# A new hand-listed order of all steps, and a branch hint ahead of the closing branch

## The chip, the cores and the metric

The kernel runs on one core of a Trainium2 chip. The metric is the device time of one execution in microseconds (us); the median of three runs of the kernel before is 583.75 us. Engines are called by the profile's short names: PE is TensorE (its matmuls), PEld its weight loads, DVE VectorE, ACT ScalarE, POOL GpSimd, SP SyncE, which here issues all DMAs.

## What is computed

The reference has two stages. The first is a linear attention with a complex decay, over 4 batches, 8 heads, 768 steps of time and 48 channels:

```python
mag = np.sqrt(a_re * a_re + a_im * a_im)
scale = np.minimum(mag, 0.999) / (mag + 1e-06)
for t in range(S):
    S_re, S_im = ar * S_re - ai * S_im + kv, ar * S_im + ai * S_re
    y[:, :, t] = np.einsum('bhd,bhde->bhe', q[:, :, t], S_re)
```

The second takes y as 3072 tokens of 384 channels through h = x @ w_in (384 to 2048), g = h * sigmoid(1.702 h), and g @ w_out (2048 to 384). All data are float32.

## The kernel before, in words

Time is cut into 12 units of 256 steps (three for each batch), each of two chunks of 128. For a unit, `prepare_part` (from L275 on) turns a into decays and rotations, by scans on DVE and tables on ACT, and multiplies them into q and k (the rotations at L207); DMAs of SP that `remap` issues (L409 to L418) then lay q and k out by heads. `attend` (from L422) is the attention of one unit. Its PE steps are, for each chunk: two **score** steps (L484), whose product DVE masks (L490); two **keys** steps, which transpose k (L499) for a copy on ACT (L502); three **mix** steps (L469), which give the attention's output; and one **z** step (L521), which gives the new state. `moe` (from L586) is the second stage for one group of one or two units: **H** steps (L615) into h_ps, a gate on ACT (L628, L630) and DVE (L632), and **O** steps (L645) into o_ps, whose sum DVE copies out (L661) for a DMA (L664). From the second group on each product of H and O is taken three times, with high and low parts of both sides, and a group has 256 columns (one unit) or 512 (two units). The weights are converted from 64-bit words on the way, at first (`convert`, `split`). Small checks of the inputs (`inspect`, `sign`, from L668) fill free time of DVE. At the end `decide` counts on PE whether all checks held; if one did not, `general()`, a slow general version, runs.

The order of the work is written out by hand. `Plan.add` numbers every step as it is described (1864 steps, with an engine, a planned duration, what it reads and writes). `Plan.order` does not plan: it returns the numbers of the string ORDER, and makes sure that no step stands ahead of one that it depends on. The planned durations therefore change nothing in the program. The loop from L838 issues the steps in that order, so that each engine, and SP's queue, has its own part of the list in the list's sequence, and each waits in it for what its steps read. An ACT table load (L841) is put in wherever the list changes tables.

The count of `decide` is loaded by all engines at L844, and L845 branches:

```python
    fits = nc.values_load(count[0:1, 0:1], ...)
    with tc.If(fits < P):
        general()
```

In the runs here all checks hold, so every engine jumps over `general()`.

Of the kernel before, what the change touches and what calls it, by code (L numbers as in the profile page):

```python
# [15 lines left out]
ENG = mybir.EngineType  # L16
# [4 lines left out]
P = 128  # L21
L = 128
QL = 32
T = 256
# [66 lines left out]
def attention_moe(ctx: ExitStack, tc: tile.TileContext, qk_in, v, a_in, w_in, w_out, qn, kn, vn, an, bn, out):  # L91
# [68 lines left out]
    def d_t(n, fast=1.0):  # L160
        return 0.07 + n * 0.00104 / fast
# [113 lines left out]
    def prepare_part(u, i, a, b, np_, mag, den, rec, sp, th, *keys):  # L275
# [34 lines left out]
        add("DVE", d_t(C) + 0.18 * C / (NR * T), rk("den"), lambda: dve.scalar_tensor_tensor(  # L310
# [111 lines left out]
    def attend(u):  # L422
# [20 lines left out]
        for c in range(2):  # L443
# [50 lines left out]
            def keys(hh, c=c, bank=bank):  # L494
                k_ps, key = bank("K", hh)

                def turn():
                    for j in range(4):
                        nc.tensor.transpose(k_ps[:, j, 0:KD], at(4 * hh + j, 1, c), ident[0:KD, 0:KD])  # L499

                add("PE", 0.27, rk(4 * c + hh), turn, r=hk[c], w=[key], work=0.85)
                add("ACT", a_t(4 * KD) - 0.12, rk(4 * c + hh), lambda: act(  # L502
                    out=kt[hh], in_=k_ps[:, :, 0:KD], func=AF.Copy
                ), r=[key], w=[f"kt{hh}"])
# [11 lines left out]
            def state(grp=None, c=c, vt=vt, reads=reads):  # L516
# [7 lines left out]
                add("PE", 0.56, rk(4 * c + 2.5), zed, r=reads["z"], w=["Z"], work=0.49, cols=E0)  # L524
# [312 lines left out]
    with tc.manual_schedule(engines={ENG.PE, ENG.Activation, ENG.DVE, ENG.Pool, ENG.SP}):  # L837
        for n in order:  # L838
            o = plan.ops[n]
            if o[5] not in (None, cur):  # L840
                nc.scalar.preload_act_table_set(o[5])  # L841
                cur = o[5]
            o[3]()
    fits = nc.values_load(count[0:1, 0:1], skip_runtime_bounds_check_because="it is only compared, never an address")  # L844
    with tc.If(fits < P):  # L845
        general()
# [256 lines left out]
```

## Time and profile before

| what | us |
|---|---|
| median of three runs (581.92, 583.75, 584.99) | 583.75 |
| the profiled execution, its own time | 580.61 |
| its span, first to last instruction | 578.9 |
| what lies around the span | 1.7 |
| first matmul to the last, in the span | 23.8 to 571.8 |
| PE busy, DVE busy, ACT busy | 531.9, 435.6, 337.6 |

A busy PE is not a PE at its peak: matmuls are pipelined, and a step that waits little still shows as busy. How long a step takes is read from the chain of waits, where a row is one piece of the chain with its start, its length and how many matmuls it has.

### The profile page before, as it was taken

How to read it: one execution, taken by the hardware profiler on the slowest of the kernel's cores; microseconds unless marked ns; L12 is line 12 of the kernel's file. 1: busy time of each engine (PE TensorE's matmuls, PEld its weight loads, DVE VectorE, ACT ScalarE, POOL GpSimd, SP SyncE). 2: the span in 40 equal slices, each digit the busy share in tenths (PEclk: the TensorE clock that was granted, in tenths of full speed). 3: DMA queues.
4: the chain of work that ended last, by engine and by line, in shares of the span. 5: the costliest groups of instructions: out<-in, count | busy, mean ns of one | idle time of the engine just before them, and what ended most of it. 6: DMA issues, size and time to landing. Idle time of an engine off the chain costs nothing.

```text
span 578.9 us, 14799 instructions
## 1 busy us (share of the span) xinstructions
PE 531.9 (92%) x6300; PEld 461.0 (80%) x6300; DVE 435.6 (75%) x739; ACT 337.6 (58%) x483; POOL 23.9 (4%) x83
## 2 busy tenths in 40 slices
PE   0369999999999998999999999999999999999995
PEld 0257877999999998988878888888888888888883
DVE  6998998999999998789889786978476734352232
ACT  7856686796978484386947836546854422233230
POOL 3001000001000000000000100000001000000000
PEclk9997999999999999899999999999999999999999
DMA  8556992163465648264372654754523372131011
GB/s 326 167 190 249 287 295 81 32 168 123 89 214 112 215 80 245 57 173 156 85 205 76 159 165 141 165 172 118 131 56 122 103 163 74 51 110 45 29 45 61
DMA packets 31530, 80.12 MB, mean 138 GB/s; under 512 B 4448, under 2 KB 8032, under 8 KB 31456
## 3 DMA queue, kind: packets, MB, share of 16 engines
q1 hardware_dynamic: 31456, 79.09, 46.5%
q8 instruction: 51, 0.84, 0.6%
q14 instruction: 23, 0.19, 0.1%
HBM read 55.44 MB, written 4.72 MB: 104 GB/s over the span
## 4 chain that ended last, share of the span: by engine, by line
PE 63%; DVE 3%; issue 1%; DMA 1%; ACT 1%; SPq 0%; DVEq 0%
PE o_ps L645 26%; PE h_ps L615 25%; PE x_ps L469 5%; PE p_ps L484 4%; PE p_ps L499 1%; PE z_ps L521 1%; DMA out_dram<-osb 1%; DVE qk L207 1%; DVE osb L661 0%; DVE qr L207 0%; DVE s L207 0%; DVE s L333 0%; DVE pm L490 0%; DVE gl L632 0%; ACT s L319 0%
## 5 line engine op out<-in xcount | busy, mean ns | idle before, releaser
L628 ACT ACTIVATE gh<-h_ps 128x512 fp32r<-128x512 f32 x88 | 52.4, 597 | 136.0 <-PE h_ps L615 96.5
L615 PE MATMUL h_ps<-xhi,hiA 128*128 128x512 f32 (+1 forms) x336 | 117.8, 351 | 0.3 <-DVE gl L632 0.3
L615 PE MATMUL h_ps<-xlo,hiA 128*128 128x512 f32 (+1 forms) x336 | 116.1, 345 | 0.0
L615 PE MATMUL h_ps<-xhi,loA 128*128 128x512 f32 (+1 forms) x336 | 116.0, 345 | 0.0
L632 DVE TENSOR_TENSOR gl<-h_ps,gh 128x512 fp32r<-128x512 f32 x88 | 60.0, 685 | 55.5 <-ACT h_ps L630 50.0
L645 PE MATMUL o_ps<-gl,hiU 128*128 128x512 f32 (+1 forms) x336 | 85.5, 353 | 1.3 <-issue 1.3
L645 PE MATMUL o_ps<-gh,hiU 128*128 128x512 f32 (+1 forms) x336 | 84.6, 351 | 0.0
L645 PE MATMUL o_ps<-gh,loU 128*128 128x512 f32 (+1 forms) x336 | 82.4, 344 | 0.0
L841 ACT ACT_TABLE_LOAD x58 | 74.4, 1283 | 1.8 <-PEq L1091 0.8
L615 PEld LDWEIGHTS h_ps<-xhi,hiA 128*128 128x128 f32 x336 | 64.2, 191 | 8.1 <-DVE gl L632 0.5
L615 PEld LDWEIGHTS h_ps<-xhi,loA 128*128 128x128 f32 x336 | 64.1, 191 | 7.7
L615 PEld LDWEIGHTS h_ps<-xlo,hiA 128*128 128x128 f32 x336 | 64.2, 191 | 7.2
L645 PEld LDWEIGHTS o_ps<-gl,hiU 128*128 128x128 f32 x336 | 56.6, 191 | 9.4 <-issue 2.1
L645 PEld LDWEIGHTS o_ps<-gh,loU 128*128 128x128 f32 x336 | 57.6, 189 | 7.8
L645 PEld LDWEIGHTS o_ps<-gh,hiU 128*128 128x128 f32 x336 | 56.6, 189 | 7.5 <-issue 0.4
L490 DVE TENSOR_TENSOR pm<-p_ps,mask 128x512 f32<-128x512 f32 x46 | 31.5, 685 | 29.8 <-PE x_ps L469 19.2
L630 ACT ACTIVATE h_ps<-h_ps 128x512 f32<-128x512 f32 x88 | 51.8, 593 | 0.0
L677 DVE TENSOR_REDUCE fit<-raw_w 128x1 f32<-128x256 f32 x96 | 37.3, 409 | 16.0 <-DMA raw_w<-in_w_out_dram 12.4
L207 DVE TENSOR_TENSOR qk<-qk,s 128x768 f32<-128x768 f32 (+1 forms) x52 | 45.7, 889 | 3.0 <-DMA qk<-in_qk_dram 2.5
L484 PEld LDWEIGHTS p_ps<-qkh 96*32 96x32 f32 x1472 | 33.4, 109 | 13.8 <-issue 10.6
L484 PE MATMUL p_ps<-qkh 96*32 96x128 f32 (+3 forms) x1472 | 38.1, 235 | 6.5 <-issue 5.9
L469 PE MATMUL x_ps<-pm,v 128*32 128x128 f32 x768 | 39.7, 281 | 2.9 <-DVE pm L490 1.6
(96 smaller groups left out, 749.3 us busy)
## 6 DMA issues: line engine op xcount, KB each, us to landing
v<-in_v_dram SPq DMA_DIRECT2D x24, 416.0 KB, 4.1
ri<-in_a_dram SPq DMA_DIRECT2D x11, 768.0 KB, 5.5
qk<-in_qk_dram SPq DMA_DIRECT2D x11, 768.0 KB, 6.4
qkh<-qr SPq DMA_DIRECT2D x22, 288.6 KB, 5.9
qkh<-qk SPq DMA_DIRECT2D x22, 288.6 KB, 4.8
raw<-in_w_in_dram SPq DMA_DIRECT2D x8, 768.0 KB, 6.6
raw<-in_w_out_dram SPq DMA_DIRECT2D x8, 768.0 KB, 5.9
raw_w<-in_w_in_dram SPq DMA_DIRECT2D x24, 256.0 KB, 2.8
```

The lines of the kernel that those rows point to most:

```text
L207: add(en, t, rank, lambda: e.tensor_tensor(out=out, in0=a, in1=b, op=alu), **kw)
L469: mm(x_ps[32 * j : 32 * j + 32, r, :], lhsT=lt, rhs=rt, start=n == 0, stop=n == len(steps) - 1)
L484: mm(ps_[to : to + QL, j, lo:L], lhsT=at(h, 1, c)[:, lo : lo + QL], rhs=at(h, 0, c)[:, lo:L], start=True, stop=True)
L490: add("DVE", d_t(CW), rk(4 * c + hh), lambda: dve.tensor_tensor(out=pm[hh], in0=bank("P", hh)[0], in1=mask, op=ALU.mult), r=[bank("P", hh) ...
L499: nc.tensor.transpose(k_ps[:, j, 0:KD], at(4 * hh + j, 1, c), ident[0:KD, 0:KD])
L615: mm(h_ps[hb][:, k * n_t : (k + 1) * n_t], lhsT=ww[:, r * T + f * P : r * T + (f + 1) * P], rhs=x[:, r, 0:n_t], start=n == 0, stop=n == last)
L628: add("ACT", a_t(CW) - 0.13, rk(s), lambda hb=hb, gb=gb: act(out=high.g(gb), in_=h_ps[hb], func=AF.Silu, scale=SLOPE), r=[f"h{hb}"], w=[f" ...
L630: add("ACT", a_t(CW) - 0.13, rk(s), lambda hb=hb: act(out=h_ps[hb], in_=h_ps[hb], func=AF.Silu, scale=SLOPE), w=[f"h{hb}"], tab=SILU, name ...
L632: add("DVE", d_t(CW), rk(s), lambda hb=hb, gb=gb: dve.tensor_tensor(out=glo[gb], in0=h_ps[hb], in1=high.g(gb).bitcast(F32), op=ALU.subtrac ...
L645: mm(o_ps[c][:, 0:n_t], lhsT=y[:, f * DM + c * P : f * DM + (c + 1) * P], rhs=x[:, k * n_t : (k + 1) * n_t], start=i == 0 and f == 0 and n ...
L677: add("DVE", d_t(CK), rk + 2, lambda x=x, op=op: dve.tensor_reduce(out=f_w[:, x, n : n + 1], in_=weights.looked_at()[:, :, 1], op=op, axis ...
L841: nc.scalar.preload_act_table_set(o[5])
```

## The change

Three things are changed. The string ORDER is another permutation of the same 1864 numbers, so every step is still issued once, with the same operands. Planned durations of three kinds of step are changed (they are read by nothing). And a branch hint is put on PE, SP, DVE and ACT between the last listed step and the load of the count, for the branch that now has the label "end"; POOL has none.

```diff
-        add("DVE", d_t(C) + 0.18 * C / (NR * T), rk("den"), lambda: dve.scalar_tensor_tensor(
+        add("DVE", d_t(C), rk("den"), lambda: dve.scalar_tensor_tensor(
...
-                add("PE", 0.27, rk(4 * c + hh), turn, r=hk[c], w=[key], work=0.85)
+                add("PE", 0.277, rk(4 * c + hh), turn, r=hk[c], w=[key], work=0.85)
...
-                add("PE", 0.56, rk(4 * c + 2.5), zed, r=reads["z"], w=["Z"], work=0.49, cols=E0)
+                add("PE", 0.615, rk(4 * c + 2.5), zed, r=reads["z"], w=["Z"], work=0.49, cols=E0)
...
-        for n in order:
+        for k, n in enumerate(order):
...
+    tc.mark_branch_hint_location("end", "LikelyTaken", (ENG.PE, ENG.SP, ENG.DVE, ENG.Activation))
     fits = nc.values_load(count[0:1, 0:1], skip_runtime_bounds_check_because="it is only compared, never an address")
-    with tc.If(fits < P):
+    with tc.If(fits < P, label="end"):
         general()
...
 ORDER = """
-80 130 0 10 185 169 101 151 15 81 82 83 132 131 84 133 85 89 86 134 2 135 93 3
+80 130 0 5 101 151 10 81 82 83 132 131 84 133 85 89 86 134 2 93 135 3 90 94
...
-1684 1681 1685 1686 1682 1687 1689 1690 1688 1694 1691 1692 1695 1862 1863 1693
+1684 1681 1685 1686 1682 1688 1689 1692 1687 1694 1693 1862 1690 1695 1863 1691
 """
```

The two lists, read as PE sees them, around the attention of unit 5 (the number of PE instructions of a step is behind the colon, matmuls and weight loads together):

```
before: mix:32 score:64 mix:64 mix:32 z:96 score:64 O:6 H:18 H:18 O:12 O:6 keys:8 H:18
after:  mix:32 score:64 mix:64 mix:32 H:18 O:6 H:18 H:18 score:64 z:96 O:12 keys:8 O:6
```

Counted over the lists: a change on PE from a score, mix or z step to an H or O step comes 32 times before and 49 times after (19 and 32 times from where the list has passed 155 us of PE work, about 200 us of the profile). Changes from keys to H or O are 36 in both. Table loads of ACT are 58 before and 54 after. The list keeps the last three O steps, the copies out and the count at its end, in another sequence of the three.

## Rows read from the trace of the kernel before

**Rows 1.** The page, part 1: busy time of PE and DVE, share of the span, instructions.

```profile
PE 531.9 (92%) x6300; PEld 461.0 (80%) x6300; DVE 435.6 (75%) x739; ACT 337.6 (58%) x483; POOL 23.9 (4%) x83
```

**Rows 2.** Busy time of each engine by stretch: the stretch, its length, then busy us (and instructions) of PE, PEld, DVE, ACT, POOL, granted clock of PE, DMA share, GB/s.

```profile
150.00:200.00 50.00, 49.22 (x721) 47.86 (x721) 47.77 (x77) 36.93 (x49) 2.53 (x11) 1.00 0.61 167
200.00:250.00 50.00, 45.59 (x824) 44.48 (x826) 42.60 (x68) 27.35 (x40) 1.10 (x5) 0.97 0.50 128
400.00:450.00 50.00, 50.00 (x547) 41.94 (x546) 33.04 (x60) 32.56 (x45) 1.85 (x5) 1.00 0.39 99
```

**Rows 3.** All waits of PE between 200 and 350 us: what waited, for what, us in total, times, longest. "issue" is time in which PE waited for nothing that the profile shows.

```profile
PE p_ps L484 <- issue: 4.8, 4, 2.6
PE o_ps L645 <- issue: 1.3, 2, 0.7
```

**Rows 4.** Of the waits of PE between 60 and 200 us, the one of this kind.

```profile
PE p_ps L484 <- issue: 1.2, 1, 1.2
```

**Rows 5.** As rows 2, of stretches that each begin and end where a wait of this kind ended. The counts behind PE and PEld, added, are the PE instructions between two such ends.

```profile
215.38:231.37 15.99, 13.41 (x253) 13.16 (x254) 14.63 (x26) 8.66 (x12) 1.10 (x5) 1.00 0.83 245
231.37:247.38 16.02, 14.91 (x256) 14.60 (x257) 10.57 (x17) 6.93 (x12) 0.00 (x0) 0.89 0.29 68
...
322.50:339.40 16.90, 16.35 (x254) 13.60 (x254) 14.24 (x26) 10.48 (x15) 0.78 (x4) 1.00 0.70 188
```

**Rows 6.** The page, part 3: the DMA queue that brings PE's instructions (packets, MB, share).

```profile
q8 instruction: 51, 0.84, 0.6%
```

**Rows 7.** As rows 2, of stretches of 256 PE instructions by start (PE's records counted in order of time, from the end of one such wait back by 256, or on by multiples of it). The first three end with a wait for issue, the last two do not.

```profile
225.90:231.37 5.47, 2.88 (x145) 2.77 (x134) 4.47 (x7) 0.00 (x0) 0.00 (x0) 1.00 0.74 272
319.16:322.50 3.34, 3.03 (x146) 2.89 (x134) 2.04 (x4) 3.30 (x6) 0.40 (x1) 1.00 0.44 96
334.31:339.40 5.09, 4.54 (x140) 3.82 (x129) 4.54 (x9) 0.91 (x2) 0.00 (x0) 1.00 0.69 227
363.59:366.15 2.56, 2.56 (x139) 2.56 (x133) 2.52 (x4) 2.54 (x4) 0.00 (x0) 1.00 0.59 155
416.78:419.46 2.68, 2.68 (x138) 2.68 (x131) 0.97 (x3) 2.65 (x4) 0.00 (x0) 1.00 0.24 89
```

**Rows 8.** The chain of waits, pieces in order of time: start, us, what, matmuls. 200 to 260 us.

```profile
228.10 0.68 PE p_ps L484 x27
228.78 2.59 issue
231.37 0.32 PE p_ps L484 x3
...
232.63 3.16 PE h_ps L615 x18
...
239.02 1.08 PE h_ps L615 x9
```

**Rows 9.** As rows 2: the one stretch after 60 us at a lower granted clock.

```profile
231.39:234.80 3.41, 3.41 (x18) 3.35 (x19) 3.07 (x5) 0.94 (x1) 0.00 (x0) 0.50 0.02 5
```

**Rows 10.** The chain of waits, 296 to 345 us. The piece at 319.44 follows a score step, the one at 332.90 an O step; the score at 318.75 follows an O step, the one at 334.36 a mix step.

```profile
318.75 0.69 PE p_ps L484 x32
319.44 1.32 PE x_ps L469 x48
...
332.90 1.46 PE x_ps L469 x48
334.36 0.56 PE p_ps L484 x32
```

**Rows 11.** The chain of waits, 408 to 460 us: H after keys, a z step, H after O, H after a score step.

```profile
409.31 2.12 PE h_ps L615 x9
...
419.05 0.67 PE z_ps L521 x48
...
422.82 2.04 PE h_ps L615 x9
...
447.03 2.26 PE h_ps L615 x9
```

**Rows 12.** The page, part 6: DMA issues, KB of each, median us from issue to landing.

```profile
v<-in_v_dram SPq DMA_DIRECT2D x24, 416.0 KB, 4.1
...
qkh<-qr SPq DMA_DIRECT2D x22, 288.6 KB, 5.9
```

**Rows 13.** The page, part 5: the table loads of ACT.

```profile
L841 ACT ACT_TABLE_LOAD x58 | 74.4, 1283 | 1.8 <-PEq L1091 0.8
```

**Rows 14.** The branch at L845 and what follows on each engine: duration in ns (least, median, most), first and last start in us.

```profile
L845 SPq EVENT_SEMAPHORE  x8: 17/17/17, 577.0 to 577.5; - x8
...
L845 POOLq COMPARE_BRANCH  x1: 45/45/45, 573.4 to 573.4; - x1
L845 PEldq COMPARE_BRANCH  x1: 4222/4222/4222, 573.4 to 573.4; - x1
...
L845 SPq COMPARE_BRANCH  x1: 45/45/45, 573.5 to 573.5; - x1
...
L845 DVEq EVENT_SEMAPHORE  x1: 21/21/21, 577.1 to 577.1; - x1
```

**Rows 15.** The end in order of time: start, us, engine, line, what.

```profile
571.10 1.69 SPq L664 DMA_DIRECT2D out_dram<-osb  x3
...
572.35 0.13 DVE L714 CAST count<-p_ps 1x1 int32<-1x1 f32 x1
```

152 rows, old and new, of the table ORDER are left out of this document.

## The prediction, on record before the change was run

> **What bounds the kernel now.** I read the page first: PE is busy for 92% of the span and DVE for 75% [rows 1]. A share over the whole span hides stages, so I cut it into stretches. Until about 200 us both are full: DVE works 47.8 of 50 us there; later it works 42.6 and then 33.0 of 50 [rows 2]. So up to 200 us a stop of PE may cost nothing, as DVE holds the pace as well; from 200 us PE alone sets the end.
>
> Then the waits of PE. Between 200 and 350 us it waits, over 150 ns at a time, for no engine and no DMA: the whole list is "issue", 4.8 + 1.3 = 6.1 us in six stops [rows 3]. There is one more before, of 1.2 us [rows 4]. Such a row names no culprit, so I counted PE's instructions from the end of one stop to the end of the next: 507, 513 and 508 [rows 5], that is twice 256, but for a few that belong to the sequencer and aren't counted. PE stops at every so many instructions, not at a step. And a queue of its own brings PE's code in 51 packets of 0.84 MB, 16 KB each, one for each 256 of the 12600 instructions [rows 1, 6]. I take the stops to be late code: a block is through before the next is there. The block ahead of a stop was short: 5.47 us with its stop of 2.59 us, or 3.34 and 5.09 us [rows 7].
>
> **What the list does to the blocks.** I give each PE step the length that its pieces have in the chain (a score step 0.69 us for 64 instructions, 48 matmuls of mix 1.32 for 96, z 0.67 for 96, H 2.04 or 1.08 for 18 [rows 8, 10, 11]) and slide a window of 256 instructions over both lists. Before, the least is 2.5 us, and by chance of phase about 9 blocks would lie under 4.2 us. After, nothing past the start-up (the first 16 us of PE work) is under 4.9 us. Attention steps that stood together now have H and O steps between them.
>
> **The sum.** From 200 us on, where PE bounds:
> - The six stops: 4.8 + 1.3 = 6.1 us go [rows 3]. The longest block with its stop took, from 200 us on, 5.47 us [rows 7], so against 4.9 some 0.6 us could stay, at the one densest place. Bounds 5.5 to 6.1; I take **-6.1**, since few blocks are that short.
> - Resuming. The score step that was cut by the stop of 2.59 us took 0.68 + 0.32 us [rows 8], one that wasn't took 0.69 [rows 10]: 0.3 us. Four of the six stops cut a score step [rows 3]: **-1.2**.
> - The clock. Right after the stop of 2.59 us the granted clock is 0.50, the 1.2 GHz level, for 3.41 us [rows 9], and 18 matmuls of H take 3.16 us [rows 8] for twice 1.08. So the dip costs between 1.0 us and half of 3.41, 1.7. PE had stood still before it; without the stop I expect no dip: **-1.4**.
> - The price: more changes between small and large matmuls. A mix step takes 1.46 us behind an O step, 1.32 behind a score step; a score 0.69 behind O, 0.56 behind a mix [rows 10]: 0.14 to enter. H takes 2.26 us behind a score step and 2.04 behind O [rows 11]: 0.22 to leave. Each further excursion costs 0.36 us. From 200 us on the list has 32 in place of 19: 13 x 0.36 = **+4.7**. Keys steps, at 2.12 against 2.04 [rows 11], are as many as before. Bounds: 13 x 0.22 = 2.9, and 17 x 0.36 = 6.1 if the early ones count too.
>
> Up to 200 us: the stop of 1.2 us [rows 4] and four more excursions (1.4 us) lie beside a DVE that is 96% busy [rows 2]. The DVE work listed ahead of each 25 us of PE work is less by 0.1 to 1.3 us than before, summed with DVE's own durations. I take **-0.6**, bounds -2.5 and +2.
>
> The moved queues. SP issues the remaps in sequence with the loads. From the second unit on, the PE work listed between a unit's last remap and the first step that reads it is at least 7.6 us after (6.5 before), and a remap lands 5.9 us after its issue [rows 12]: covered; if the list is early by 2 us more, PE waits for the difference, unit by unit. The first unit's v loads move behind its q and k loads and around its first remap; a load lands in 4.1 us [rows 12], the z step that reads it comes after the remaps, which take as long: 0, at worst +2 at the start, within the bound above. POOL only swaps neighbouring edge fills and copies, which wait for DVE: 0. ACT drops 4 table loads of 1.28 us [rows 13], 5.1 us on an engine busy 58% [rows 1]: 0 on the path. The planned durations are read by nothing: 0. The last three O steps change places among themselves, the copy out of the last still closes: 0.
>
> The end. After the branch at 573.4 us PE's takes 4.22 us, where POOL's, without a long jump, takes 45 ns; SP's next instruction comes at 577.0, 3.5 us after its branch, DVE's at 577.1 [rows 14]. I read this as waiting for the code behind `general()`. A hint can't wait less than its head start. SP's stands behind its last issue (571.10 + 1.69 = 572.8), DVE's behind the cast (572.35 + 0.13 = 572.5) [rows 15]; their branches are at 573.5 or just before. That is 0.7 to 0.9 us. PE and ACT could gain more, but then SP and DVE are late next: SP has eight waits of its own behind the branch [rows 14]. **-0.8**; bounds 0 (the trace has no hint, and its own issue is of the order of 45 ns) and -3.5.
>
> Together -6.1 - 1.2 - 1.4 + 4.7 - 0.6 - 0.8 = **-5.4 us**. The profiled execution took 580.61 us, which would become 575.2. It lies 3.1 us under the median of 583.75, whose runs spread over 3 us. Taken from the median: **578.4 us**.
>
> **A rule against it.** Every stop here is at a multiple of 256 instructions [rows 5]. The Trainium skill, in "Runtime: NRT & Kernel Launch", section "Instruction fetch mechanics", says the contrary: crossing such a block is mostly hidden, as instructions are dispatched slower than they are filled in. By that rule the stops would be something else and stay, and the sum is that of the first rival. The trace disagrees where blocks are short, by 0.3 to 2.6 us at each stop.
>
> **Rivals.**
> 1. *The stops stay* (slower). Closeness doesn't decide; the code's packets come late behind other DMA traffic, wherever the block boundary then lies. For it: two blocks of 2.56 and 2.68 us passed without a stop, and DMAs were busy 0.24 to 0.59 there, against 0.44 to 0.74 at the three stops [rows 7]. Against it: no block with a stop took over 5.47 us there [rows 7], so a later boundary must be later still to show. Then 6.1, 1.2 and 1.4 us aren't won and the excursions are paid: +4.7 - 0.6 - 0.8 = +3.3, 587.1 us. It decides if fetches take over 7 us. Chance 0.11.
> 2. *The excursions eat it.* A lone z step, which now often stands between H and O steps, has no row before that shows its price; if each excursion costs 0.6 us rather than 0.36, early ones included, 17 x 0.6 = 10.2 stands against 6.1 + 1.2 + 1.4 + 0.8 = 9.5: +0.7, 584.4 us. Against it: z is as short as score, and its neighbours are the same. With parts of this, no change that shows: 0.23.
> 3. *The early part gains too.* If DVE's stretch up to 200 us gets shorter by the bound of 2.5, and the hint saves 3.5: -6.1 - 1.2 - 1.4 + 4.7 - 2.5 - 3.5 = -10.0, 573.8 us. Against it: DVE's work is the same. Chance 0.16.
>
> That the hint does nothing would move the sum to -4.6, within the forecast.
>
> **How the numbers follow.** The forecast, -3 to -8 us, has 0.50. About 0.5% (2.9 us) is what a measurement of this kernel can tell from no change. Faster by more: the forecast and rival 3, 0.66; within it: rival 2, 0.23; slower: rival 1, 0.11. The range reaches from beyond rival 3 to rival 2: 573.0 to 584.5 us leaves out rival 1 and a tail of the third, less than 2 in 10.
>
> **What would show it.** In the changed kernel's profile: waits of PE for issue between 200 and 350 us under 1 us in all; no stretch at clock 0.50 behind them; more pieces of H and O at 2.26, and of mix at 1.46 us; SP's first wait behind the branch about 0.8 us nearer to it, PE's branch far under 4.2 us. The prediction is wrong if waits for issue stay at 256 instructions, if new waits of PE for DVE or ACT of over 3 us in all appear after 200 us, or if the first 200 us hold over 2 us more or less PE work.

## The result, and the profile after

The changed kernel takes 568.47 us (median of 4 runs, 567.57 to 570.37), the kernel before 583.23 (4 runs, 581.92 to 584.99): a ratio of 0.975, 95% interval 0.971 to 0.979, 14.8 us less. The forecast was 5.4 us less, with a range down to 573.0 us: the direction was right, but the gain was 2.7 times the forecast and the time lay below the range. The profiled execution took 567.6 us for 580.61, its span 565.8 for 578.9. So 13.1 us can be followed through the two traces; the rest is that the profiled run of before lay further below its median.

Busy time hardly moved against [rows 1, 6], though the span shrank by 13 us. Parts 1 and 3 of the page after:

```profile
PE 532.5 (94%) x6300; PEld 457.1 (81%) x6300; DVE 433.2 (77%) x739; ACT 333.3 (59%) x479; POOL 23.9 (4%) x83
...
q8 instruction: 50, 0.82, 0.6%
```

**The stops** are nearly gone. From 200 to 350 us the list of PE's waits, six stops of 6.1 us before [rows 3], is empty. From 60 to 200 us it has one stop, for the 1.2 us of [rows 4]:

```profile
PE p_ps L484 <- issue: 0.5, 1, 0.5
```

From 60 us to PE's last step no stretch has a granted clock under 1.00, where before had 3.41 us at 0.50 [rows 9].

**The price of excursions** came as worked out. The chain of waits after, 406 to 425 us (start, us, what): z behind H takes 0.81 where it took 0.67 behind a score step [rows 11], mix 1.46, and O behind attention 2.26 or 2.27 (9 matmuls of H behind another large step take 2.04).

```profile
404.78 2.04 PE h_ps L615 x9
406.82 0.81 PE z_ps L521 x48
407.63 0.82 PE p_ps L484 x29
408.45 2.27 PE o_ps L645 x9
...
420.35 1.46 PE x_ps L469 x48
421.81 0.56 PE p_ps L484 x32
422.37 0.44 PE x_ps L469 x16
422.81 2.26 PE o_ps L645 x9
```

**The early part**, which I had at -0.6 us, is where much of the rest is. Busy time by stretch as in [rows 2], first the kernel before, then after:

```profile
30.00:60.00 30.00, 24.71 (x387) 20.27 (x380) 26.44 (x41) 18.35 (x26) 2.40 (x5) 0.89 0.67 241
60.00:110.00 50.00, 46.80 (x546) 39.81 (x545) 46.38 (x68) 36.86 (x50) 1.38 (x5) 1.00 0.57 174
110.00:200.00 90.00, 89.01 (x1293) 86.60 (x1293) 86.75 (x133) 68.48 (x91) 5.37 (x15) 1.00 0.55 149
```

```profile
30.00:60.00 30.00, 26.18 (x401) 20.87 (x399) 28.16 (x44) 21.69 (x30) 3.71 (x7) 0.94 0.74 227
60.00:110.00 50.00, 49.26 (x582) 42.70 (x580) 48.73 (x72) 39.99 (x53) 1.85 (x5) 1.00 0.61 201
110.00:200.00 90.00, 89.50 (x1346) 86.59 (x1348) 88.14 (x138) 67.04 (x91) 3.69 (x15) 1.00 0.53 145
```

The third busy figure is DVE's: 159.57 of 170 us before, 165.03 after. DVE stood 10.4 us in these stretches and now stands 5.0. What stood shows in the waits of PE, ACT and DVE from 24 to 110 us, of the kernel before (kt is the transposed k, pm the masked scores, raw the weights as they are loaded):

```profile
PE z_ps L521 <- ACT kt L502: 2.4, 1, 2.4
PE x_ps L469 <- DVE pm L490: 1.6, 1, 1.6
PE x_ps L469 <- ACT x L527: 1.3, 1, 1.3
PE p_ps L484 <- issue: 1.2, 1, 1.2
PE p_ps L499 <- ACT kt L502: 1.0, 1, 1.0
```

```profile
ACT raw L225 <- DMA raw<-in_w_out_dram: 5.7, 1, 5.7
```

```profile
DVE qk L207 <- DMA qk<-in_qk_dram: 2.5, 1, 2.5
DVE pm L490 <- PE p_ps L484: 1.9, 2, 1.7
```

and after:

```profile
PE x_ps L469 <- DVE pm L490: 1.6, 1, 1.6
PE x_ps L469 <- DVE st L440: 0.9, 1, 0.9
...
PE z_ps L521 <- ACT kt L502: 0.6, 1, 0.6
```

```profile
ACT raw L225 <- DMA raw<-in_w_out_dram: 0.3, 1, 0.3
```

Before, ACT stood 5.7 us in front of a weight load (f4, the fifth of 16; L225), with the copies of kt behind it in its queue; z waited 2.4 us for kt, mix 1.3 us for the copy behind it, and PE ran at half its clock from 43.66 us on, for 6.83 us, 5.53 of them busy. After, the clock was half earlier and for 3.42 us, all busy. Half of the difference in busy time is 1.1 us, my estimate of what the clock has in the early gain. Before, then after:

```profile
43.66:50.49 6.83, 5.53 (x72) 4.49 (x70) 6.73 (x11) 3.07 (x6) 2.14 (x5) 0.50 0.67 255
```

```profile
37.92:41.34 3.42, 3.42 (x69) 2.66 (x69) 2.93 (x5) 0.85 (x1) 1.57 (x3) 0.50 0.67 225
```

**The end.** The rows that answer to [rows 14], and the hint's own:

```profile
L846 SPq EVENT_SEMAPHORE  x8: 17/17/17, 563.8 to 564.4; - x8
...
L846 PEldq COMPARE_BRANCH  x1: 393/393/393, 563.2 to 563.2; - x1
...
L846 SPq COMPARE_BRANCH  x1: 70/70/70, 563.3 to 563.3; - x1
```

```profile
L1100 SPq BRANCH_PREFETCH_HINT  x1: 60/60/60, 0.8 to 0.8; - x1
...
L1100 PEldq BRANCH_PREFETCH_HINT  x1: 50/50/50, 0.9 to 0.9; - x1
```

PE's branch takes 0.39 us for 4.22, SP goes on 0.5 us behind its branch for 3.5, and the span ends 2.6 us behind it for 5.5. The hint is not where the source line stands, between the last step and the load of the count: it is ahead of every listed step, at 0.8 to 0.9 us, 562 us ahead of the branch.

To put the 13.1 us in their places I matched the traces step by step: for each list, when did PE begin the step that has so much listed PE work ahead of it in the list (with the lengths of the prediction)? Below, "a work of 62" means the step that has 62 us of PE work ahead of it. The experiments' traces stand beside them; what was changed in each is told with it.

```
PE work listed ahead, us     0     15     30     62    150    200    300    508  | span
before                    23.8   52.0   67.0  105.0  196.3  254.5  359.9  571.3  | 578.9
after                     23.6   47.9   64.3   98.3  190.7  242.8  347.0  561.1  | 565.8
early part new            23.4   46.1   62.5   96.9  189.9  247.3  353.7  565.1  | 572.6
later part new            23.1   51.4   66.4  104.0  195.2  247.2  351.4  564.5  | 572.2
one conversion moved      23.1   48.5   64.5  104.6  195.5  252.2  359.4  570.8  | 578.3
old list, padded          23.3   50.9   65.9  101.3  193.9  246.0  349.0  560.6  | 568.8
combination               23.5   47.9   63.9   98.3  190.7  242.6  346.3  558.5  | 563.3
```

After is 5.6 us ahead at a work of 150 (196 us in before), 10.2 at PE's end and 13.1 at the span's: early part -5.6, from there on -4.6, end -2.9. The prediction had -0.6, -4.0 and -0.8. The early gain is larger than the spread of runs: PE reaches a work of 150 at 194 to 199 us in the four traces whose early part is the old one, untouched, and at 190 to 193 us in the ten with the new one.

In the experiments' series the runs of before spread by 1.5 to 2.2%, and the ratios leave out runs more than 1.5% above a kernel's fastest, so medians of all runs stand beside them.

### The profile page after: what moved, and what is told of

It is laid out like the page before. It is cut to its first block, busy times and chain, and to the rows that moved or that the text cites. A ratio compares the mean times of both kernels' runs of the same rounds, so it can differ in the third digit from the quotient of the medians.

```text
span 565.8 us, 14819 instructions
## 1 busy us (share of the span) xinstructions
PE 532.5 (94%) x6300; PEld 457.1 (81%) x6300; DVE 433.2 (77%) x739; ACT 333.3 (59%) x479; POOL 23.9 (4%) x83
## 4 chain that ended last, share of the span: by engine, by line
PE 75%; DVE 12%; DMA 5%; ACT 3%; issue 2%; SPq 1%; POOL 0%; DVEq 0%; ACTq 0%; POOLq 0%
PE o_ps L645 31%; PE h_ps L615 30%; PE x_ps L469 6%; PE p_ps L484 4%; PE z_ps L521 2%; PE p_ps L499 2%; DMA qk<-in_qk_dram 1%; DVE qk L207 1%; DMA raw<-in_w_out_dram 1%; DVE s L367 1%; DMA raw_w<-in_w_out_dram 1%; DVE valU L232 1%; DVE valU L229 1%; DVE s L349 1%; DVE valA L229 1%
## 5 line engine op out<-in xcount | busy, mean ns | idle before, releaser
L469 PE MATMUL x_ps<-pm,v 128*32 128x128 f32 x768 | 37.8, 275 | 1.7 <-DVE pm L490 1.6
L484 PE MATMUL p_ps<-qkh 96*32 96x128 f32 (+3 forms) x1472 | 36.3, 236 | 0.7 <-issue 0.5
```

The source lines that it names most:

```text
L469: mm(x_ps[32 * j : 32 * j + 32, r, :], lhsT=lt, rhs=rt, start=n == 0, stop=n == len(steps) - 1)
L484: mm(ps_[to : to + QL, j, lo:L], lhsT=at(h, 1, c)[:, lo : lo + QL], rhs=at(h, 0, c)[:, lo:L], start=True, stop=True)
```

## The experiments

**The hint alone.** The old list, with the hint.

```diff
+    tc.mark_branch_hint_location("end", "LikelyTaken", (ENG.PE, ENG.SP, ENG.DVE, ENG.Activation))
...
+    with tc.If(fits < P, label="end"):
```

> The old list with the hint alone. The two traces put the new kernel's last instruction 2.6 us behind the branch, before it was 5.5 us. If the hint alone does that, this run is 2.9 us under the kernel before (580.3 for 583.2) and PE's closing branch takes about 0.4 us in place of 4.2. If the prediction's reasoning holds, that a hint gives no more than its head start, 0.8 us. If the end is shorter because of the new list's last steps, nothing.

578.28 us for 581.23; ratio 0.996 (0.993 to 1.000). The span ends 2.7 us behind the branch (577.0 to 579.7), PE's branch takes 398 ns. The trace shows 2.8 us at the end, as the first theory says; the times alone barely tell the gain from nothing.

**The new list alone.** The changed kernel without the hint.

```diff
-    tc.mark_branch_hint_location("end", "LikelyTaken", (ENG.PE, ENG.SP, ENG.DVE, ENG.Activation))
...
-    with tc.If(fits < P, label="end"):
+    with tc.If(fits < P):
```

> The new list without the hint. If list and hint add up, 2.9 us above the kernel after, that is 11 to 12 us under the kernel before (571 to 572), with the closing branch at 4.2 us on PE again. The prediction's sum gave the list alone -4.6 us (578.6).

571.15 us for 581.23; ratio 0.983 (0.979 to 0.987), 10.1 us less. PE's branch takes 4478 ns again. Within the spread of the runs, list and hint add up.

**Two halves of the list.** Here and below the new string is written short, as it is made from the two lists.

```diff
-ORDER = old
+ORDER = new[:350] + [n for n in old if n not in new[:350]]   # the early part new
+ORDER = old[:349] + [n for n in new if n not in old[:349]]   # the later part new
```

> The new list's first 350 steps (63 us of PE work, up to about 100 us), then the rest in the old list's sequence; no hint. Theory: the start-up and the early part gain by themselves, and the gain is kept to the end, as it is PE's time and not covered by DVE: -5 to -6 us (577 to 578), and the six stops of 200 to 350 us are all there (about 6 us of waits for issue). Rival, the prediction's: DVE holds the pace up to 200 us, so the early gain is eaten again: -0.6 us, within 0.3% of before. Then the early gain of the full change would come from the later steps' places.

> The old list's first 349 steps, then the rest in the new list's sequence; no hint. Theory: only what the prediction's sum has for the stretch from 200 us on, -4 to -5 us (578.5), and the start-up's 6.8 us at the half clock and its wait of PE for kt of 2.4 us are as before. Rival: the later steps carry the whole gain, -10 us or more. Waits of PE for issue from 200 us on under 1 us under both, if closeness makes the stops.

Early part new: 574.69 us; ratio 0.991 (0.987 to 0.995), medians 6.5 us apart. PE is 8.1 us ahead at a work of 62 and still 6.2 at its end, with all six stops there (200 to 350 us):

```profile
PE p_ps L484 <- issue: 4.7, 4, 2.6
PE o_ps L645 <- issue: 1.9, 2, 1.0
```

Later part new: 576.52 us; ratio 0.993 (0.990 to 0.997), medians 4.7 us apart, no wait for issue from 200 to 350 us. So the early gain exists by itself, is as large as the later one, and DVE does not eat it: the claim that DVE holds the pace falls. The later part is close to what the sum said (-4.0).

**One conversion moved.** Is it the 5.7 us wait of ACT?

```diff
-... 192 191 193 ... 181 187 ... 196 ... 197 24
+... 192 191 193 ... 181 187 ... 196 ... 197 21 24   # 21: ACT's copy of raw f4, 24: DVE's last step of f4
```

> The old list with one conversion moved: ACT's copy of the raw weights f4, which waits 5.7 us for its load ahead of the copies of kt, goes behind the attention's output copies (steps 191, 193, 304, 290, 181, 197), and the DVE step that reads it right behind it. Theory: this is the bigger part of the start-up's gain. PE's wait for kt of 2.4 us goes and much of the 6.8 us at the half clock; the PE work of the first 15 us is done 2.5 to 4 us sooner (at 48 to 49.5 us for 52.0), and what is left at the end is -2 to -4 us (579 to 581 for 583). Rival: the new list's other moves in the start-up make it, DVE's and SP's order above all: under 1 us, as ACT's wait only moves elsewhere.

582.30 us for 583.04; ratio 1.007 (1.003 to 1.010): no gain. The start-up does what the theory said: 3.5 us ahead at a work of 15, kt's wait 0.3 us. But PE then waits elsewhere, and by a work of 62 only 0.4 us is left. PE's waits from 24 to 200 us:

```profile
PE o_ps L645 <- DVE valU L232: 4.7, 1, 4.7
PE x_ps L469 <- DVE pm L490: 4.6, 2, 2.9
```

valU, converted weights of w_out, waits for the load f10. Here it is issued at 62.1 us, 1.0 us sooner than before, but needs 8.4 us to land where before it needed 6.1 (the load's row, before and here):

```profile
raw<-in_w_out_dram SPq DMA_DIRECT2D x1, 768.0 KB, 6.1
```

```profile
raw<-in_w_out_dram SPq DMA_DIRECT2D x1, 768.0 KB, 8.4
```

The load that takes f4's buffer (f8) is not what is late: it lands at 52.6 us for 51.9. And f10 is later still in a trace where no step was moved (the hint alone: 10.0 us to land, PE's wait 4.5 us). So the theory is half right: that wait costs what it seemed to in the start-up, but removing it alone gains nothing, by 12 runs. Where the 3.5 us went is not shown.

**Loads or steps.** Which half of the early part is it?

```diff
-ORDER = old
+ORDER = old, with steps 0 to 79 (weight loads, conversions) at the new list's places   # loads alone
+ORDER = old, with the rest of new[:350] in the new sequence, steps 0 to 79 as in old   # steps alone
```

> The old list, in which the 16 weight loads of the start and their 64 conversion steps stand where the new list has them (by the work listed ahead of them); 7 other steps move with them. Theory: the early gain comes from the lead between a load and its first conversion (f4: 3.4 us of PE work between its issue and ACT's conversion in the old list, 10.3 in the new one), so that neither ACT nor DVE stands for a late load: -4 to -6 us (577 to 579), PE's waits for kt and valU under 1.5 us in all. Rival: the sequence of the attention's and the decay's steps makes it; under 1.5 us here. The six stops of 200 to 350 us are there in both.

> The other half: the first 350 steps in the new list's sequence, but for the weight loads and their conversions, which stand where the old list has them. Theory of the leads: no gain, within 1.5 us of before, with a wait of ACT or DVE for raw of 4 us or more and PE behind it. Rival: -4 to -6 us.

Neither theory holds: both halves lose. Loads alone: 594.35 us for 582.11, ratio 1.020 (1.015 to 1.024). Steps alone: 585.90, ratio 1.007 (1.003 to 1.011). Waits of PE and DVE from 24 to 110 us in the first,

```profile
PE o_ps L645 <- DVE valU L232: 2.7, 1, 2.7
PE h_ps L615 <- DVE valA L232: 2.7, 1, 2.7
PE x_ps L469 <- ACT x L527: 2.5, 1, 2.5
```

```profile
DVE qk L207 <- DMA qk<-in_qk_dram: 4.8, 1, 4.8
```

and of ACT and DVE in the second:

```profile
ACT raw L225 <- DMA raw<-in_w_out_dram: 4.8, 1, 4.8
```

```profile
DVE valA L226 <- DMA raw<-in_w_in_dram: 3.4, 1, 3.4
```

Each half brings waits of 2.5 to 4.8 us that the whole new list doesn't have. My reading is that four raw buffers, one queue of loads and three engines that take their work in sequence have to fit each other. What is shown is that neither half has the early gain alone; which few of the displaced steps would do is open.

**The old list, padded.** Is a stop tied to the steps or to the block's end?

```diff
+        for _ in range(32):
+            mm(h_ps[0][:, 0:1], lhsT=ident, rhs=ident[:, 0:1], start=True, stop=True)
```

> The old list, with 32 one-column matmuls on PE at the start, where PE waits for its first data anyway: 128 instructions more (matmuls and weight loads), so that every block boundary lies 128 instructions earlier in the list. Theory of blocks of 256 that come late: no stop is left at the six old steps; the short blocks are then those that begin at 179, 210, 225, 243 and 333 us in the trace of before (2.50, 2.53, 2.79, 2.56 and 2.69 us long), and stops of 0.5 to 2.8 us stand at the end of three to five of them; about 3 to 8 us in all, the time within 3 us of before. Rival, closeness itself (the steps that follow too closely make PE's queue run dry, wherever a block ends): the stops stay at the same steps with the same lengths.

571.89 us for 583.04; ratio 0.991 (0.987 to 0.995), so 5 us by the ratio and 11 between the medians; the spans of the two traces are 10.1 us apart, 8.3 of it from a work of 150 on (366.7 us to PE's end for 375.0). For that stretch the sum had 6.1 + 1.2 + 1.4 = 8.7 us for the stops and what follows them, and 0.75 us of stops is left. Waits for issue from 60 to 350 us, and PE's counts from the end of the first stop to that of the second (1146 + 1145: nine times 256, but for 13 not counted):

```profile
PE p_ps L484 <- issue: 1.0, 1, 1.0
PE x_ps L469 <- issue: 0.8, 1, 0.8
```

```profile
179.26:242.01 62.75, 62.00 (x1146) 60.83 (x1145) 59.71 (x99) 39.43 (x58) 2.66 (x10) 1.00 0.58 158
```

No stop is left at the six old steps, so the rival falls. Counted through (PE's records in order of time, the sequencer's included), all 52 stops past 60 us in the 18 traces end at a number that leaves 193 when divided by 256, padded or not. How many stops there would be I had wrong: two, not three to five, and a gain of 5 to 11 us was in neither theory. The phase of the old list was an unlucky one.

**Fewer transfers.** The loads of 90 of the 96 weight blocks that are looked at left out (`inspect`, L668 on).

```diff
-        add("SP", 0.8, rk, lambda: dma(
+        add("SP", 0.8, rk, lambda: n % 16 == 0 and dma(
```

> The old list with 90 of the 96 loads of the weights' checks left out (most blocks of the weights are then not checked; the reductions run on what lies there). DVE, ACT and PE do the same work, the DMAs carry less from 200 us on. The prediction's first rival (code comes late behind other transfers): the waits for issue of 200 to 350 us fall from 6.1 us to under 2. Theory that a block needs some 5 us to come, whatever else is moved: at least 4 us of them stay.

584.36 us for 583.04; ratio 1.011 (1.003 to 1.019). The DMA share from 250 to 350 us fell from 0.53 and 0.51 to 0.42 and 0.38, and the stops from 200 to 350 us stay, 6.0 us:

```profile
PE p_ps L484 <- issue: 4.8, 4, 2.1
PE o_ps L645 <- issue: 1.2, 2, 0.8
```

Only three of them lie behind 250 us, though, 2.4 us for 1.6 before; from 200 to 250 us the share is 0.50 in both, so the other three, 3.6 us for 4.4, say nothing. From 250 us on, then, fewer transfers do not bring the code sooner. What makes it late can be narrowed down: the packets of PE's code queue, one for each block in sequence, for some of the shorter blocks of three traces.

```
kernel     block, us   stop, us   next code packet starts: behind block's start / ahead of its end, us
before       2.55        0           -0.93 / 3.49
before       3.05        0            0.34 / 2.70
before       3.75        0.75         1.51 / 2.24
before       4.03        1.10         0.85 / 3.18
before       5.47        2.59         3.01 / 2.46
padded       3.28        0            0.55 / 2.73
padded       4.41        0.98         1.90 / 2.51
padded       5.30        0.75         2.70 / 2.60
after        6.29        0.50         3.89 / 2.40
```

The same holds in all 18 traces, which have 828 block ends past 60 us. At the 52 with a stop, PE goes on 2.2 to 3.2 us behind the packet's start, and without the stop it would have been through the block at most 2.6 us behind it. At the 776 without a stop, the packet started at least 2.2 us ahead of the block's end. That is what shows the stops to be late code. No block of over 5.8 us of its own stopped PE, but 69 blocks under 5 us passed, as their packet came early. What delays a packet's start is open.

**The new list, padded.** Is the new list lucky too? The changed kernel, with the same two lines of padding.

> The kernel after with the 128 instructions of padding. Closeness theory: in the new list no 256 PE instructions past the start-up take under 4.9 us wherever a block begins, so waits of PE for issue past 60 us stay under 1.5 us in all and the time within 1.5 us of the kernel after (567 to 570). Rival: the new list is only lucky in its phase, as the padded old list was; then 3 us or more of such waits, 571 or more.

566.89 us for 582.11; ratio 0.974 (0.970 to 0.978). No wait for issue over 0.15 us past 60 us at all. In the two phases tried the new list has 0.5 and 0 us of stops past 60 us, the old one 7.2 and 1.7.

**The combination**: three of the edits above together.

```diff
-ORDER = old
+ORDER = new[:350] + [n for n in old if n not in new[:350]]   # and the padding, and the hint
```

> The new list's first 350 steps, then the old sequence, with the 128 instructions of padding at the start and with the hint. If the parts add up: early part -5.5 to -6.5, blocks -7 to -9 (what the padded old list gained from 150 us on), hint -2.9, and no further excursions between small and large matmuls to pay for: -15 to -18 us against the kernel before (565 to 568), which is level with the kernel after or up to 3 us under it. Rival: the gains overlap (the stop at 90 us is in both the first two), -13 us or less.

565.26 us for 582.11; ratio 0.972 (0.968 to 0.977), 16.9 us less. It is below the changed kernel (568.47, another series) and 1.6 below the padded new list of its own series, whose interval it overlaps: it is faster than before for certain; that it is faster than the changed kernel, by 1.6 to 3.2 us, is not clear of the noise. It pays for fewer excursions (212.2 us for the work from 300 to 508, the changed kernel 214.1) and has one stop of 0.5 us.

**The hint's place.** First right before the load, where I had taken it to be.

```diff
+    tc.no_sync_barrier()
     tc.mark_branch_hint_location("end", "LikelyTaken", (ENG.PE, ENG.SP, ENG.DVE, ENG.Activation))
```

> The new list with the hint where the prediction took it to be: behind each engine's last listed step, right before the load of the count, 0.7 to 0.9 us ahead of the branch (in the kernel after it stands 560 us ahead, at the very start of each engine's program). The prediction's reasoning, a hint gives back no more than its head start: PE's branch still takes over 3 us and the span ends about 4.5 to 4.9 us behind the branch (2.6 in the kernel after, 5.5 without a hint). Rival: its place doesn't matter; PE's branch takes about 0.4 us and the span ends 2.6 us behind it.

568.77 us for 583.04, ratio 0.983 (0.975 to 0.991), too wide to tell it from the early hint; the trace does:

```profile
L847 PEldq COMPARE_BRANCH  x1: 4567/4567/4567, 565.1 to 565.1; - x1
```

```profile
L1101 PEldq BRANCH_PREFETCH_HINT  x1: 45/45/45, 560.6 to 560.6; - x1
...
L1101 SPq BRANCH_PREFETCH_HINT  x1: 55/55/55, 564.6 to 564.6; - x1
```

It gives nothing, not even on PE, where it stood 4.5 us ahead: the end comes 5.7 us behind the branch, so the 0.8 us that the prediction's reasoning gave it do not come either. Then further ahead, inside the list, one run each.

```diff
         for k, n in enumerate(order):
+            if k == K:   # 1829, 1735, 962, 222: 15, 60, 300, 480 us of PE work ahead of the end
+                tc.no_sync_barrier()
+                tc.mark_branch_hint_location("end", "LikelyTaken", (ENG.PE, ENG.SP, ENG.DVE, ENG.Activation))
+                tc.no_sync_barrier()
```

> The new list with the hint some 60 us of PE work ahead of the end. Right before the count's load (PE 4.5 us, ACT 6.3, DVE 1.6, SP 0.9 us ahead of the branch) it gave nothing, at the very start 2.9 us. If what matters is a head start longer than the few us that the code takes to come, 60 us are as good as 560: PE's branch about 0.4 us, the span ends 2.6 us behind it. Rival: what the hint brings in does not stay, or a hint in the middle of a stream is overtaken by the blocks that follow it: PE's branch over 3 us, 5.5 us to the end.

> The same with the hint some 15 us of PE work ahead of the end. By a head start of a few us: 2.6 us from the branch to the end. If more than 15 us are needed: 5.5 us.

> The new list with the hint some 300 us of PE work ahead of the end. With 60 us of lead PE's and ACT's branches were served (next instruction within 0.5 us), DVE's and SP's not (4.0 us); with 15 us only PE's. Theory: the lead that an engine needs is counted in its own instructions, and SP and DVE run few (31 and 59 between the hint and the branch at 60 us). At 300 us DVE has over 300 between and SP over 150: DVE's next instruction comes within 0.7 us of its branch, SP's as well, and the span ends 2.6 us behind it. Rival: for DVE and SP only the very start serves; then 4 us on both, and the end 5.5 to 6 us behind the branch.

> The same some 480 us ahead of the end, past the start-up but not at the program's start. Theory of the lead: all five engines within 0.7 us, 2.6 us from the branch to the end. Rival as before: DVE and SP 4 us.

They took 571.90, 569.67 (before, once: 580.17), 566.02 and 568.52 us (577.04). From their traces, for each engine: us from its branch to its next instruction, and in brackets the hint's lead in us and in the engine's own instructions.

```
hint                 PE                  ACT                DVE                SP            branch to end
none (before)    4.3                 3.0                3.7                3.5                5.5
before the load  4.6 (4.5, 27)       3.1 (6.3, 3)       3.8 (1.5, 3)       3.4 (0.9, 2)       5.7
15 us            0.4 (20, 165)       3.0 (19, 12)       4.2 (21, 22)       4.0 (20, 6)        6.0
60 us            0.4 (65, 562)       0.5 (68, 48)       4.1 (65, 59)       4.0 (63, 31)       6.0
300 us           0.5 (313, 6294)     0.5 (313, 290)     0.6 (312, 434)     0.5 (313, 209)     2.6
480 us           0.5 (504, 11823)    0.5 (504, 516)     0.6 (505, 780)     0.5 (501, 353)     2.6
start (after)    0.5 (562)           0.5 (562)          0.6 (562)          0.5 (562)          2.6
```

In these single runs a hint serves its engine or it doesn't, there is no partial gain, and the end only moves when all four are served; with some unserved it came 6.0 us behind the branch, 0.5 us later than without a hint. The start is not needed, a long lead is. The lead in time alone doesn't sort the cases (PE is served at 20 us, DVE and SP not at 65); whether own instructions or the code's blocks count is not settled (ACT is served at 48 instructions, DVE not at 59).

## Why the prediction was right or wrong

- **Right: what the stops are.** Late code at multiples of 256 instructions: the padding moved all of them, and each falls where the code packet starts at most 2.6 us ahead of need. The Trainium skill ("Runtime: NRT & Kernel Launch", "Instruction fetch mechanics") says that crossing such a block is mostly hidden. By count it is: 39 of 46 block ends past 60 us in before pass without a stop. The other seven cost 7.3 us [rows 3, 4] and what follows them. After, one is left, of 0.5 us, so the first rival, in which the stops stay, did not come.
- **Right in size: the later part.** -6.1 - 1.2 - 1.4 + 4.7 = -4.0 was the sum, -4.6 us is in the traces, 4.7 between the medians with only this part new. Its two sides came as well, by the padded old list: from a work of 150 on that takes 366.7 us with 0.75 us of stops in it, for 375.0 before, and the new one 370.4, so its 13 further excursions cost some 4.5 us for 4.7.
- **Wrong: the early part, -0.6 for -5.6 us.** The step that failed is "as DVE holds the pace as well", and with it a term that was put near nothing: the -0.6 is taken there, not added up from rows. I read it from one stretch, 150 to 200 us [rows 2], where DVE stands 2.2 of 50 us, and took it for all that lies before. From 30 to 110 us DVE stood 7.2 of 80. And a busy share of 94% is no limit: DVE itself waited for loads and for PE, and a list that fits those better can win what it stood, here 5.4 of 10.4 us. With only the early part new, the gain is kept to the end (6.2 us there). The bound of -2.5 was too small as well. The wait for f4 and the half clock behind it were in the trace of before; I never asked what the start-up's stops cost PE. Which of the moved steps make the gain stays open, as both halves of the early part lose alone. The prediction named this as what would prove it wrong: over 2 us more or less PE work in the first 200 us.
- **Wrong: the end, -0.8 for -2.9 us.** The step that failed is where the hint stands. "A hint can't wait less than its head start" was reasoned for a hint behind SP's last issue; put there, it gives nothing at all. In the changed kernel it stands 562 us ahead, and no engine is late next. My bound of -3.5 held.
- **The range** took the third rival as its edge (-10.0 us), with -2.5 for the early part. With the measured terms, -5.6 - 4.6 - 2.9, the sum is -13.1, which from the median of 583.75 is 570.7 us, outside it.

## What to carry to other kernels

When PE stops for "issue" at even distances of 256 instructions, try some padding instructions where PE is idle before rewriting the order: here that alone was worth 5 to 11 us. The order without short blocks had next to no stops in both phases tried. A busy share near 95% on another engine is not a pace: read from the waits what that engine stands for, in every stretch, before costing a gain at nothing. Put a hint for a far branch early (here 300 us ahead served every engine, 65 us did not), and look in the trace at where each engine has it.

## What the runs showed of the hardware that was not expected

- 128 more PE instructions at the start, which cost no time there, took 5 us (by the ratio) to 11 us (between medians) off the old list.
- A far branch costs an engine 3.0 to 4.6 us; with a hint 300 us or more ahead 0.4 to 0.6, and the hint itself 45 to 65 ns. The Trainium skill ("Runtime: NRT & Kernel Launch", "Instruction fetch mechanics") says that a taken branch to code that is not at hand has to wait for a fetch; the rows agree, and an early hint takes that wait away.
- What a code packet needs: PE went on 2.2 to 3.2 us behind the start of the packet that it stood for, in all 52 stops of 18 traces.
- One and the same weight load (f10) took 6.1, 7.4 and 10.0 us to land in three traces of the old list (before, fewer transfers, hint alone), with nothing changed ahead of it but the hint, and PE's wait for valU at about 70 us was 0.7, 2.1 and 4.5 us. Such waits may be part of why runs of one kernel spread by 2%; that isn't shown.
